# Table functions in halves between copies, loads and transposes by token pairs, doubled coefficients, a split last group: one change to a two-head kernel

## The chip, the core and the metric

The kernel runs on one core of a Trainium2 chip. The metric is the time of one execution in microseconds of the device. A run of the kernel before is the median of its executions; one of its executions was taken with the hardware profiler, and all rows below come from that one.

## The reference, cut to what matters

Two independent heads work on 2048 tokens of width 448, and their outputs are put side by side.

```python
# head A: attention of each token over 8 tokens, 2 apart, 16 heads of 28
q, k, v = (x @ wqkv).reshape(B, S, 3, H, Dh) ...
idx = pos[:, None] - off[None, :]            # off = 0, 2, ..., 14; below 0 is masked
logits = einsum("bhsd,bhswd->bhsw", q, k[idx]) * scale
a = einsum("bhsw,bhswd->bhsd", softmax(logits), v[idx]).reshape(B, S, D) @ wo
# head B: a diagonal complex state space, P = 448
Lam_bar = exp(exp(log_dt) * Lam);  B_bar = ((Lam_bar - 1) / Lam)[:, None] * Bmat
h[t] = Lam_bar * h[t-1] + B_bar @ x[t]
b = 2 * real(Cmat @ h) + x * Dskip
out = concatenate([a, b], -1)
```

## The kernel before, in words

**Head A.** Partition p holds the 16 neighbouring tokens 16p to 16p+15 (`J = 16`; "token j" below is the j-th of each partition). x is loaded into `xnA` (in the buffer u1) in four groups of four tokens, 448 KB each, by `load_x` (L104). `g_xta` (L288) transposes a group on TensorE, 16 transposes into two PSUM banks, and VectorE copies each bank to `xTA` (L296). `proj(t, j)` (L300) makes q (t = 0), k (1) or v (2) of one token: 4 matmuls (L303) and a ScalarE copy (L307). The 14 tokens before a partition's first come from the partition before by DMAs from SBUF to SBUF, `halo` (L545). `logits` (L436) works for one half of the tokens (hf = 1: tokens 8 to 15) and two of the 8 offsets at a time: a product of q and k over 7168 elements (`mul`, L445), and sums over the 28 columns (`half` L448, `quarter` L451, after every second one `rest` L454 to L457). `softmax` (L469) has a first and a second part. `pv_mul` (L503) multiplies the weights with v, four tokens and one offset at a time, into one of 7 buffers; `av` (L511) adds over offsets and transposes on TensorE, 16 matmuls with the identity (L519) into four PSUM banks, which are copied out after the eighth offset (L526, L528). `wo_j` (L531) is the output projection of one token. The four groups of tokens run from 12..15 down to 0..3; `wo_j` of a group runs between the `av` of the next.

**Head B.** The recurrence is cut into 256 chunks of 8 steps (`T = 8`), real and imaginary parts on two halves of the partitions. `params_in` and `params1` to `params3` (L218 to L266) compute powers of Lam_bar from three small loads (`prow`) and one of Dskip. `blocks` (L202) multiplies the pattern `dup` of two unit matrices with coefficients that are broadcast over the last axis: `build_R` makes one of 7 rotation matrices R (128x896), `build_G` the two that scale B, which lie in R[5] and R[6]. `tables` (L282) makes cos and sin of the chunk angle for 1792 elements: three VectorE passes in float32 scratch in u1 (L283, L196, L197), then Sin, Abs and Sin on ScalarE (L198 to L200). `b_weights` (L311), `b_x` (L320; the copies of even steps on VectorE, L327, of odd ones on ScalarE) and `c_weights` (L333) prepare operands. `ssm_in` (L353) runs the 8 steps in a chunk, for the first four of seven column groups (hf = 0) and then the last three (hf = 1). It begins with step 0, which reads the last xT copy that `b_x` makes. `scan_mul` (L372), `scan_pe` (L379), `scan_run` (L391), `scan_mul`, `scan_pe`, `scan_out` rotate into the frame of a chunk, scan over chunks and rotate back. `ssm_mix` (L403) spreads the result over the steps and `ssm_out` (L416) projects it.

**Order.** Each engine runs its instructions in the order in which the program issues them; nothing moves them afterwards. TensorE's order is the text's. Most VectorE work of head A and of the parameters goes through a list, `todo`, as pairs of a cost and a function (`add`). `pe(cost)` and `dve(cost)` keep two running sums, `load[0]` for TensorE and `load[1]` for VectorE, and `pump` takes work off the list while VectorE's sum is below TensorE's. So the costs written in the text decide in front of which b_x copies, scans and rotations a product lands. `need` takes off all that is before an item. At the start, 44 matmuls of the identity (L134) run while x is on its way. The PSUM pool has 8 banks, given out in turn. Loads, halos and stores are issued by SP in the text's order; the small parameter loads by ScalarE.

```python
def pump(lead=0.0):
    while todo and load[1] < load[0] + lead and (todo[0][2] is None or todo[0][2]()):
        pop()
```

Of the kernel before, what the change touches and what calls it, by code (L numbers as in the profile page):

```python
# [19 lines left out]
KT = 112  # L20
T = 8
# [15 lines left out]
def kernel(  # L37
# [29 lines left out]
    def bank(dt=F32):  # L67
        return psum.tile([128, 512 if dt == F32 else 1024], dt, tag="b", name="b")
# [34 lines left out]

    def load_x(jg):  # L104
        SP.dma_start(xnA[:, 4 * jg:4 * jg + 4, :], xA_r[:, 4 * jg:4 * jg + 4, :])

    def half_rows(src):
        return src.rearrange("(t i) d -> i t d", i=HS)

    load_x(3)  # L110
    load_w(1)
    load_x(2)
    load_x(1)
    load_w(0)
    load_x(0)
    prow = const.tile([3 * NT, 2, HS], BF16, tag="prow")
# [15 lines left out]
    warm = bank()  # L132
    for _ in range(44):
        PE.matmul(warm[:, 0:128], ident[:], ident[:], start=True, stop=True)  # L134
# [20 lines left out]
    todo = []  # L155
    load = [8.0, 8.0]

# [17 lines left out]
    def pe(cost):  # L175
        load[0] += cost
        pump()

    def dve(cost):
        load[1] = max(load[1], load[0]) + cost  # L180
# [5 lines left out]
    def tt(o, a_, b_, op):  # L186
        V.tensor_tensor(o, a_, b_, op)
        return o
# [6 lines left out]
    def sincos(sin_out, cos_out, y, tmp):  # L195
        V.tensor_scalar(tmp, y, 1.0, MAGIC, ALU.mult, ALU.add)  # L196
        V.scalar_tensor_tensor(tmp, tmp, -MAGIC, y, ALU.add, ALU.subtract)  # L197
        ACT.activation(sin_out, tmp, ACTF.Sin, scale=-2 * PI * SHR)  # L198
        ACT.activation(tmp, tmp, ACTF.Abs)
        ACT.activation(cos_out, tmp, ACTF.Sin, bias=hpib[:], scale=-2 * PI * SHR)  # L200

    def blocks(o, c, n):  # L202
        shp = (128, n, 2, HS)
        V.tensor_tensor(o.rearrange("p m (a b) -> p m a b", a=2), dup.unsqueeze(1).to_broadcast(shp),  # L204
                        c.unsqueeze(3).to_broadcast(shp), ALU.mult)

# [5 lines left out]
    nr, t0, den, gre, gim = [pt_(n) for n in ("nr", "t0", "den", "gre", "gim")]  # L212
    coef = const.tile([128, T - 1, NT, 2], BF16, tag="coef")
    cg = pt_("cg", (128, NT, 2))
    cgb = const.tile([128, 2, NT, 2], BF16, tag="cgb")
    kkb = kk.unsqueeze(2).to_broadcast(PW)
# [24 lines left out]

    def params2():
        tt(sn[:], sn[:], rk[:], ALU.mult)
        V.tensor_copy(coef[0:HS, :, :, 1], sn[0:HS, 0:T - 1])
        V.tensor_scalar(coef[HS:128, :, :, 0], sn[HS:128, 0:T - 1], -1.0, None, ALU.mult)
        tt(cs[:], cs[:], rk[:], ALU.mult)
        V.tensor_copy(coef[0:HS, :, :, 0], cs[0:HS, 0:T - 1])
        V.tensor_copy(coef[HS:128, :, :, 1], cs[HS:128, 0:T - 1])

    def params3():  # L250
        a1, b1 = cs[:, 0], sn[:, 0]
        V.tensor_scalar(nr[:], a1, -1.0, None, ALU.add)
        tt(gre[:], nr[:], lre, ALU.mult)
        tt(t0[:], b1, lim, ALU.mult)
        tt(gre[:], gre[:], t0[:], ALU.add)
        tt(gre[:], gre[:], den[:], ALU.mult)
        tt(gim[:], b1, lre, ALU.mult)
        tt(t0[:], nr[:], lim, ALU.mult)
        tt(gim[:], gim[:], t0[:], ALU.subtract)
        tt(gim[:], gim[:], den[:], ALU.mult)  # L260
        V.tensor_copy(cg[0:HS, :, 0], gre[0:HS])
        V.tensor_copy(cg[0:HS, :, 1], gim[0:HS])
        V.tensor_scalar(cg[HS:128, :, 0], gim[HS:128], -1.0, None, ALU.mult)
        V.tensor_copy(cg[HS:128, :, 1], gre[HS:128])
        V.tensor_copy(cgb[:, 0], cg[:])
        tt(cgb[:, 1], cg[:], cgb[:, 0], ALU.subtract)  # L266

    def build_G():
        blocks(G.rearrange("p r t n -> p (r t) n"), cgb.rearrange("p r t a -> p (r t) a"), 2 * NT)

# [6 lines left out]

    ftab = u1.bitcast(F32)
    yy = ftab[:, 0:NT * NC].rearrange("p (t c) -> p t c", t=NT)
    tm = ftab[:, NT * NC:2 * NT * NC].rearrange("p (t c) -> p t c", t=NT)  # L280

    def tables():  # L282
        V.tensor_tensor(yy, iot.unsqueeze(1).to_broadcast((128, NT, NC)),  # L283
                        fT.unsqueeze(2).to_broadcast((128, NT, NC)), ALU.mult)
        sincos(tab[:, 1], tab[:, 0], yy, tm)


    def g_xta(jg):  # L288
        for k2 in range(2):
            tp = bank(BF16)  # L290
            tpv = tp[0:KT].rearrange("p (k j n) -> p k j n", k=2, j=4)
            for kk_ in range(2):
                for jj in range(4):
                    kt = 2 * k2 + kk_
                    PE.transpose(tpv[:, kk_, jj, :], xnA[:, 4 * jg + jj, KT * kt:KT * (kt + 1)], ident[:])
            V.tensor_copy(xTA[:, 2 * k2:2 * k2 + 2, 4 * jg:4 * jg + 4, :], tpv)  # L296
            dve(0.69)
            load[0] += 0.45

    def proj(t, j):  # L300
        ps = bank()
        for kt in range(4):
            PE.matmul(ps[:, 0:D], xTA[:, kt, j, :], wts[:, t, kt, :], start=(kt == 0), stop=(kt == 3))  # L303
        src = ps[:, 0:D].rearrange("p (h d) -> p d h", h=H)
        dst = (q_s[:, :, j * H:(j + 1) * H] if t == 0 else
               k_s[:, :, HALO + j, :] if t == 1 else v_s[:, HALO + j])
        ACT.copy(dst, src)  # L307
        pe(0.76)

# [186 lines left out]
    out_a = out[0].rearrange("(p j) n -> j p n", j=J)  # L496
    steps = [(n_, jg, s) for n_, jg in enumerate((3, 2, 1, 0)) for s in range(W)]
    count = [0, 0]

    def pv_of(i):  # L500
        return late[:, 1792 * (i % NPV):1792 * (i % NPV + 1)].rearrange("p (j d h) -> p j d h", j=JG, d=DH)

    def pv_mul(i):  # L503
        _, jg, s = steps[i]
        V.tensor_tensor(pv_of(i), attn[:, s, JG * H * jg:JG * H * (jg + 1)].rearrange("p (j h) -> p j h", h=H)  # L505
                        .unsqueeze(2).to_broadcast((128, JG, DH, H)), v_s[:, 2 * s + JG * jg:2 * s + JG * jg + JG], ALU.mult)
        count[0] += 1
# [3 lines left out]
    def av(i):  # L511
        n_, jg, s = steps[i]
        if s == 0:
            accs[n_] = [bank() for _ in range(4)]
        acc = accs[n_]
        pvf = pv_of(i).rearrange("p j d h -> p j (d h)")
        for kt in range(4):
            for jj in range(JG):
                PE.matmul(acc[kt][0:KT, jj * 128:(jj + 1) * 128], pvf[:, jj, KT * kt:KT * (kt + 1)], ident[:],  # L519
                          start=(s == 0 and jj == 0), stop=(s == W - 1 and jj == JG - 1))  # L520
        count[1] += 1
        if s == W - 1:
            for kt in range(4):
                o, a_ = oTs[n_ % 3][:, kt], acc[kt][0:KT].rearrange("p (j n) -> p j n", j=JG)
                if n_ == 3 and kt % 2 == 1:
                    V.tensor_copy(o, a_)  # L526
                else:
                    ACT.copy(o, a_)  # L528
        pe(0.92)

    def wo_j(n_, jj):  # L531
        j = JG * (3 - n_) + jj
        ps = bank()
        for kt in range(4):
            PE.matmul(ps[:, 0:D], oTs[n_ % 3][:, kt, jj, :], wo_p[:, kt, :], start=(kt == 0), stop=(kt == 3))  # L535
        ya = outp.tile([128, D], BF16, tag="yo")
        if n_ == 3 and jj % 2 == 1:
            V.tensor_copy(ya[:], ps[:, 0:D])
        else:
            ACT.copy(ya[:], ps[:, 0:D])  # L540
        SP.dma_start(out_a[j, :, 0:D], ya[:])
        pe(0.76)
# [6 lines left out]

    g_xta(3)  # L550
    params_in()
    add(1.6, params1)
    add(1.2, params2)
    add(2.5, params3)
    has_G = add(2.0, build_G)
    has_R = [add(1.0, lambda: build_R(0))]
    for j in (15, 14, 13, 12):
        proj(1, j)
    g_xta(2)
    for j in (11, 10, 9):  # L560
        proj(1, j)
    g_xta(1)
    for j in (8, 7, 6):
        proj(1, j)
    g_xta(0)
    has_tab = add(6.2, tables)
    has_D = add(0.6, build_D)
    for j in range(15, 7, -1):
        proj(0, j)
# [12 lines left out]
    for k in range(1, T - 1):  # L582
        has_R.append(add(1.0, lambda k=k: build_R(k)))
    halo(lambda lo, hi, a_, b_: v_s[lo:hi, a_:b_])
# [11 lines left out]
    for j in range(T):  # L596
        if j == 1:
            need(has_R[0])
        ssm_in(0, j)
    need(has_tab)  # L600
    scan_mul(0)
    for t2 in range(4):
# [27 lines left out]
    has_wo = add(0.0, wo_load)  # L630
    for i in range(32):
        add(1.09, lambda i=i: pv_mul(i), lambda: count[0] < count[1] + NPV)

# [8 lines left out]

    for i in range(32):
        while count[0] <= i:
            pop()
        pump(7.0)
        av(i)
        n_, _, s = steps[i]
        if n_ > 0 and s % 2 == 1:
            wo_j(n_ - 1, s // 2)  # L650
    for jj in range(JG):
        wo_j(3, jj)

# [28 lines left out]
```

## Time and profile before

| what | value |
|---|---|
| median of 3 runs (lowest, highest) | 183.68 us (183.63, 184.69) |
| profiled execution: own time | 183.74 us |
| its span, first to last instruction | 182.0 us |
| mean granted TensorE clock | 0.979 |
| TensorE: projections L303, 192 matmuls | 41.5 us busy |
| TensorE: L519, 512 matmuls | 32.3 us |
| VectorE: products L445, 8 of 3.89 us | 31.1 us |
| VectorE: L505, 32 of 1.09 us | 32.2 us |
| ScalarE: L198, L199, L200 | 1.70, 1.70, 1.79 us |

The stages, by the start of what begins them: first projection at 7.88 us, tables (L283) at 22.77, first product (L445) at 35.01, first `ssm_in` matmul at 62.78, first C transpose (L340) at 79.94, last `ssm_out` matmul at 133.57, first L519 at 135.83, last L535 at 178.49, end at 182.0.

How to read the profile: a row of the waits names the engine and line that waited, the engine and line that released it, the sum in us, how often, and the longest. A row of the timeline gives start, busy time, engine, line, operation, operands and shapes, and in brackets the idle time ahead of it with its releaser. A row of stages gives for each engine the busy time and the number of instructions; then the granted TensorE clock (1.00 is full rate), the busy share of the DMA engines and GB/s.

### The profile page before, as it was taken

How to read it: one execution, taken by the hardware profiler on the slowest of the kernel's cores; microseconds unless marked ns; L12 is line 12 of the kernel's file. 1: busy time of each engine (PE TensorE's matmuls, PEld its weight loads, DVE VectorE, ACT ScalarE, POOL GpSimd, SP SyncE). 2: the span in 40 equal slices, each digit the busy share in tenths (PEclk: the TensorE clock that was granted, in tenths of full speed). 3: DMA queues.
4: the chain of work that ended last, by engine and by line, in shares of the span. 5: the costliest groups of instructions: out<-in, count | busy, mean ns of one | idle time of the engine just before them, and what ended most of it. 6: DMA issues, size and time to landing. Idle time of an engine off the chain costs nothing.

```text
span 182.0 us, 3801 instructions
## 1 busy us (share of the span) xinstructions
PE 167.4 (92%) x1596; PEld 123.2 (68%) x1596; DVE 150.3 (83%) x172; ACT 95.8 (53%) x180; POOL 2.8 (2%) x22
## 2 busy tenths in 40 slices
PE   6968996599999899999999899999959999999992
PEld 7745652256667688887886565656539988888860
DVE  1358992399997899999999999999999999996031
ACT  2093538977787544443468955447720224426151
POOL 3000000000000000000000010000000000000000
PEclk9999999789999999999999999999996999999999
DMA  5999940059469100000000002111222001011113
GB/s 169 314 261 262 338 86 0 0 116 171 73 132 199 26 4 0 0 4 0 0 4 0 0 25 72 58 50 50 79 78 86 4 25 58 32 48 52 54 50 101
DMA packets 13135, 14.01 MB, mean 77 GB/s; under 512 B 4527, under 2 KB 12223, under 8 KB 12991
## 3 DMA queue, kind: packets, MB, share of 16 engines
q1 hardware_dynamic: 13047, 13.77, 29.6%
q8 instruction: 12, 0.20, 0.4%
q14 instruction: 5, 0.04, 0.1%
q10 hardware_dynamic: 71, 0.01, 0.0%
HBM read 6.89 MB, written 3.67 MB: 58 GB/s over the span
## 4 chain that ended last, share of the span: by engine, by line
DVE 41%; PE 39%; DMA 10%; ACT 4%; issue 3%; SPq 1%; ACTq 0%; DVEq 0%
PE b L519 17%; PE b L303 12%; DVE u L445 11%; DMA u<-in_B_x_dram 7%; PE b L535 7%; DVE u L448 4%; DVE R L204 4%; DVE l L451 3%; DMA prow<-in_B_log_dt_dram 3%; DVE u L394 2%; PE b L325 2%; PE b L315 2%; DVE l L454 2%; DVE wbuf L375 1%; DVE wbuf L376 1%
## 5 line engine op out<-in xcount | busy, mean ns | idle before, releaser
L303 PE MATMUL b<-wbuf,u 112*128 112x448 bf16 x192 | 41.5, 363 | 5.9 <-ACT q_s L307 3.7
L445 DVE TENSOR_TENSOR u<-q_s,k_s 128x7168 bf16<-128x7168 bf16 x8 | 31.1, 3888 | 6.7 <-ACT q_s L307 6.5
L519 PEld LDWEIGHTS <-k_s 128*112 128x112 bf16 x512 | 32.0, 135 | 4.1 <-DVE k_s L505 2.4
L519 PE MATMUL b<-ident,k_s 128*112 128x128 bf16 x512 | 32.3, 225 | 2.3 <-DVE k_s L505 2.3
L303 PEld LDWEIGHTS <-u 112*128 112x128 bf16 x192 | 18.1, 100 | 22.4 <-issue 5.9
L505 DVE TENSOR_TENSOR k_s<-u,v_s 128x1792 bf16<-128x1792 bf16 x32 | 32.2, 1089 | 0.4 <-PE b L519 0.4
L360 PE MATMUL b<-xT,BT 112*128 112x256 bf16 x224 | 26.9, 272 | 0.8 <-DVE xT L327 0.8
L367 ACT CAST u<-b 128x512 bf16<-128x512 f32 (+1 forms) x32 | 15.6, 535 | 18.4 <-PE b L366 14.8
L360 PEld LDWEIGHTS <-BT 112*128 112x128 bf16 x224 | 21.7, 98 | 4.0 <-DVE xT L327 0.9
L420 PE MATMUL b<-Cw,u 128*128 128x448 bf16 x112 | 23.8, 352 | 0.0
L540 ACT CAST ya<-b 128x448 bf16<-128x448 f32 x14 | 7.5, 538 | 18.0 <-PE b L535 13.3
L448 DVE TENSOR_TENSOR u<-u 128x3584 bf16<-128x3584 bf16 x8 | 16.2, 2023 | 0.2
L420 PEld LDWEIGHTS <-u 128*128 128x128 bf16 x112 | 10.5, 98 | 7.5
L424 ACT CAST yo<-b 128x448 bf16<-128x448 f32 x16 | 8.6, 537 | 11.5 <-PE b L422 8.7
L535 PE MATMUL b<-u,q_s 112*128 112x448 bf16 x64 | 14.1, 352 | 0.0
L528 ACT CAST q_s<-b 112x512 bf16<-112x512 f32 x14 | 7.2, 596 | 11.7 <-PE b L519 11.7
L411 ACT CAST u<-b 128x512 bf16<-128x512 f32 (+1 forms) x28 | 13.1, 558 | 0.2 <-PE b L410 0.2
L307 ACT CAST v_s<-b 128x448 bf16<-128x448 f32 x16 | 8.5, 532 | 3.3 <-PE b L303 3.3
L307 ACT CAST k_s<-b 128x448 bf16<-128x448 f32 x16 | 7.9, 552 | 4.4 <-PE b L303 4.4
L410 PE MATMUL b<-u,R 128*128 128x255 bf16 x49 | 9.5, 272 | 0.7 <-ACT u L401 0.7
L307 ACT CAST q_s<-b 128x448 bf16<-128x448 f32 x16 | 8.2, 535 | 3.5 <-PE b L303 3.5
L408 PE MATMUL b<-u,ident 128*128 128x512 bf16 (+1 forms) x28 | 9.9, 353 | 0.0
(119 smaller groups left out, 184.1 us busy)
## 6 DMA issues: line engine op xcount, KB each, us to landing
u<-in_A_x_dram SPq DMA_DIRECT2D x4, 448.0 KB, 6.3
u<-in_B_x_dram SPq DMA_DIRECT2D x2, 896.0 KB, 16.9
out_dram<-yo SPq DMA_DIRECT2D x16, 112.0 KB, 1.7
out_dram<-ya SPq DMA_DIRECT2D x16, 112.0 KB, 1.7
wbuf<-in_A_wqkv_dram SPq DMA_DIRECT2D x3, 392.0 KB
k_s<-k_s SPq DMA_DIRECT2D x1, 784.0 KB
v_s<-v_s SPq DMA_DIRECT2D x1, 784.0 KB
k_s<-k_s SPq DMA_DIRECT2D x1, 588.0 KB
```

Of the source, the lines that this page charges most:

```text
L303: PE.matmul(ps[:, 0:D], xTA[:, kt, j, :], wts[:, t, kt, :], start=(kt == 0), stop=(kt == 3))
L307: ACT.copy(dst, src)
L360: PE.matmul(ps[:, i * NC:(i + 1) * NC], BT[:, kt, t, :], xT[:, kt, j, :], start=(kt == 0 and i == 0), stop=(kt == 3 and j == 0 and i == le ...
L367: ACT.copy(Z[:, pr_[0]:pr_[0] + n, j, :], ps[:, 0:n * NC].rearrange("p (t c) -> p t c", t=n))
L408: PE.matmul(ps[:, 0:n * NC], ident[:], Z[:, sl, j, :], start=True, stop=False)
L411: ACT.copy(Z[:, sl, j, :], ps[:, 0:n * NC].rearrange("p (t c) -> p t c", t=n))
L420: PE.matmul(ps[:, 0:D], Z[:, t, j, cols], Cw[:, t, :], start=(t == 0), stop=False)
L445: V.tensor_tensor(pr[:], qv, kv, ALU.mult)
L448: V.tensor_tensor(pr[:, :, 0:14, :], pr[:, :, 0:14, :], pr[:, :, 14:28, :], ALU.add)
L505: V.tensor_tensor(pv_of(i), attn[:, s, JG * H * jg:JG * H * (jg + 1)].rearrange("p (j h) -> p j h", h=H) .unsqueeze(2).to_broadcast((128, ...
L519: PE.matmul(acc[kt][0:KT, jj * 128:(jj + 1) * 128], pvf[:, jj, KT * kt:KT * (kt + 1)], ident[:], start=(s == 0 and jj == 0), stop=(s == W ...
L535: PE.matmul(ps[:, 0:D], oTs[n_ % 3][:, kt, jj, :], wo_p[:, kt, :], start=(kt == 0), stop=(kt == 3))
```

## The change

- **Loads.** `load_x(lo, hi)` takes any range of tokens. Tokens 14, 15 come first, then the k weights, 12, 13, then 8 to 11 and 4 to 7, the q weights, and 0 to 3: five loads instead of four.
- **Transposes by pairs.** `g_xta(jp)` does two tokens: 8 transposes in one bank and one copy. Eight calls stand between the projections. The warming matmuls go from 44 to 34.
- **Tables.** The scratch moves from u1 into the table itself and R[1..4]. The VectorE passes stay whole. The three functions are cut into a part of 1024 and one of 768 elements, and the six go into a list, `acts`, from which `proj` takes one after every second copy.
- **Doubled coefficients.** `coef` and `cgb` hold each coefficient twice, side by side, and `blocks` reads them, `dup` and the output with a last axis of two. R[0] is now built ahead of G.
- **Last group.** The last four tokens become two groups of two. `pv_mul` of these works on 896 elements, `av` makes 8 matmuls into two banks, and `wo_j` of the group before is spread accordingly.
- **Costs.** The starting sums of `load` go from 8 to 6, `build_R` from 1.0 to 0.5 and 0.6, `build_G` from 2.0 to 1.0, `pv_mul` to 0.15+0.235 per token.

On VectorE the order changes at two places behind this. Before, the last xT copy (step 0) comes ahead of the product of the first offsets for hf = 0; now it comes after it. Before, `scan_run` of hf = 1 comes after a `quarter`; now after a product.

```diff
-    load_x(3)
+    load_x(14, 16)
     load_w(1)
-    load_x(2)
-    load_x(1)
+    load_x(12, 14)
+    load_x(8, 12)
+    load_x(4, 8)
     load_w(0)
-    load_x(0)
+    load_x(0, 4)
...
-    for _ in range(44):
+    for _ in range(34):
...
-    load = [8.0, 8.0]
+    load = [6.0, 6.0]
...
     def blocks(o, c, n):
-        shp = (128, n, 2, HS)
-        V.tensor_tensor(o.rearrange("p m (a b) -> p m a b", a=2), dup.unsqueeze(1).to_broadcast(shp),
-                        c.unsqueeze(3).to_broadcast(shp), ALU.mult)
+        shp = (128, n * 2, HS // 2, 2)
+        V.tensor_tensor(o.rearrange("p m (a b e) -> p m a b e", a=2, e=2),
+                        dup.rearrange("p a (b e) -> p a b e", e=2).unsqueeze(1).to_broadcast((128, n, 2, HS // 2, 2)),
+                        c.unsqueeze(3).to_broadcast((128, n, 2, HS // 2, 2)), ALU.mult)
...
-    coef = const.tile([128, T - 1, NT, 2], BF16, tag="coef")
+    coef = const.tile([128, T - 1, NT, 2, 2], BF16, tag="coef")
...
-    ftab = u1.bitcast(F32)
-    yy = ftab[:, 0:NT * NC].rearrange("p (t c) -> p t c", t=NT)
-    tm = ftab[:, NT * NC:2 * NT * NC].rearrange("p (t c) -> p t c", t=NT)
+    yy = tab.rearrange("p a t c -> p (a t c)").bitcast(F32).rearrange("p (t c) -> p t c", t=NT)
+    tm = R[:, 1:5].rearrange("p k t n -> p (k t n)").bitcast(F32).rearrange("p (t c) -> p t c", t=NT)
...
-        sincos(tab[:, 1], tab[:, 0], yy, tm)
+        V.tensor_scalar(tm, yy, 1.0, MAGIC, ALU.mult, ALU.add)
+        V.scalar_tensor_tensor(tm, tm, -MAGIC, yy, ALU.add, ALU.subtract)
+        for t in (slice(0, 4), slice(4, NT)):
+            acts.append(lambda t=t: ACT.activation(tab[:, 1, t], tm[:, t], ACTF.Sin, scale=-2 * PI * SHR))
+            acts.append(lambda t=t: ACT.activation(tm[:, t], tm[:, t], ACTF.Abs))
+            acts.append(lambda t=t: ACT.activation(tab[:, 0, t], tm[:, t], ACTF.Sin, bias=hpib[:], scale=-2 * PI * SHR))
...
+    def g_xta(jp):
+        tp = bank(BF16)
+        tpv = tp[0:KT].rearrange("p (k j n) -> p k j n", k=4, j=2)
+        for kt in range(4):
+            for jj in range(2):
+                PE.transpose(tpv[:, kt, jj, :], xnA[:, 2 * jp + jj, KT * kt:KT * (kt + 1)], ident[:])
+        V.tensor_copy(xTA[:, :, 2 * jp:2 * jp + 2, :], tpv)
+        dve(0.69)
+        load[0] += 0.45
...
         ACT.copy(dst, src)
+        count[2] += 1
+        if acts and count[2] % 2 == 0:
+            acts.pop(0)()
         pe(0.76)
...
-    steps = [(n_, jg, s) for n_, jg in enumerate((3, 2, 1, 0)) for s in range(W)]
-    count = [0, 0]
+    groups = ((12, 4), (8, 4), (4, 4), (2, 2), (0, 2))
+    steps = [(n_, s) for n_ in range(len(groups)) for s in range(W)]
...
-    g_xta(3)
+    g_xta(7)
     params_in()
...
-    has_G = add(2.0, build_G)
-    has_R = [add(1.0, lambda: build_R(0))]
-    for j in (15, 14, 13, 12):
-        proj(1, j)
+    has_R = [add(0.5, lambda: build_R(0))]
+    has_G = add(1.0, build_G)
+    for jp in (6, 5, 4, 3):
+        proj(1, 2 * jp + 3)
+        proj(1, 2 * jp + 2)
+        g_xta(jp)
+    proj(1, 7)
     g_xta(2)
-    for j in (11, 10, 9):
-        proj(1, j)
-    g_xta(1)
-    for j in (8, 7, 6):
-        proj(1, j)
-    g_xta(0)
+    proj(1, 6)
     has_tab = add(6.2, tables)
     has_D = add(0.6, build_D)
-    for j in range(15, 7, -1):
+    proj(0, 15)
+    g_xta(1)
+    proj(0, 14)
+    g_xta(0)
+    for j in range(13, 7, -1):
         proj(0, j)
...
-        has_R.append(add(1.0, lambda k=k: build_R(k)))
+        has_R.append(add(0.6, lambda k=k: build_R(k)))
...
-    for i in range(32):
-        add(1.09, lambda i=i: pv_mul(i), lambda: count[0] < count[1] + NPV)
+    for i in range(len(steps)):
+        add(0.15 + 0.235 * groups[steps[i][0]][1], lambda i=i: pv_mul(i), lambda: count[0] < count[1] + NPV)
```

## The prediction, made before the changed kernel ran

> **What bounds the kernel now.** I read the busy times, then the slices, the waits, the chain, and last the stages around each wait.
>
> ```profile
> PE 167.4 (92%) x1596; PEld 123.2 (68%) x1596; DVE 150.3 (83%) x172; ACT 95.8 (53%) x180; POOL 2.8 (2%) x22
> ...
> PEclk9999999789999999999999999999996999999999
> ```
>
> TensorE is busy in 92% of the span. Two slices have a low clock. The waits say what stands before both:
>
> ```profile
> DVE u L445 <- ACT q_s L307: 6.5, 1, 6.5
> PE b L303 <- ACT q_s L307: 3.7, 1, 3.7
> PE b L519 <- DVE k_s L505: 2.3, 1, 2.3
> PE b L360 <- DVE xT L327: 0.8, 1, 0.8
> ```
>
> The 6.5 and 3.7 us are one event. ScalarE works on the table functions and copies nothing:
>
> ```profile
> 24.82 1.09 DVE L196 TENSOR_SCALAR u<-u 128x1792 f32<-128x1792 f32 x1
> 28.01 1.70 ACT L198 ACTIVATE tab<-u 128x1792 bf16<-128x1792 f32 x1 [3.44 <-DVE u L197]
> 33.16 1.81 ACT L307 CAST q_s<-b 128x448 bf16<-128x448 f32 x4
> 35.01 3.89 DVE L445 TENSOR_TENSOR u<-q_s,k_s 128x7168 bf16<-128x7168 bf16 x1 [6.50 <-ACT q_s L307]
> ```
>
> From 62.78 to 133.57 TensorE runs almost without a gap, and VectorE beside it; from 135.83 on the chain is TensorE. In stages of one microsecond a gap in TensorE's work shows its second price:
>
> ```profile
> 35.00:36.00 1.00, 1.00 (x4) 0.37 (x3) 0.99 (x1) 1.00 (x3) 0.00 (x0) 0.50 0.00 0
> ...
> 137.00:138.00 1.00, 1.00 (x11) 1.00 (x11) 1.00 (x2) 0.00 (x0) 0.00 (x0) 0.50 0.31 76
> ```
>
> The column before the last two is the granted clock. Summed over its slices, each of the two stretches loses 1.70 us (0.29+0.50+0.50+0.41; 0.09+3x0.50+0.11). They follow idle times of 3.7 and 2.26 us; idle times of 2.06 us (from 12.2) and 0.8 us (62.0) are followed by none.
>
> Two places will decide. The first is the start of the state-space stage; the second is its second half:
>
> ```profile
> 62.03 0.69 DVE L327 COPY xT<-b 112x1024 bf16<-112x1024 bf16 x1 [0.60 <-PE b L325]
> 62.64 3.88 DVE L445 TENSOR_TENSOR u<-q_s,k_s 128x7168 bf16<-128x7168 bf16 x1
> 62.78 3.67 PE L360 MATMUL b<-xT,BT 112*128 112x256 bf16 x32 [0.79 <-DVE xT L327]
> ...
> 98.40 0.55 DVE L376 TENSOR_TENSOR wbuf<-u,tab 128x768 bf16<-128x768 bf16 x1
> 98.86 1.08 DVE L451 TENSOR_TENSOR l<-u 128x1792 bf16<-128x1792 bf16 x1
> 99.87 1.84 DVE L394 TENSOR_TENSOR_SCAN u<-rk,b 128x256 bf16<-128x256 f32 x3
> 102.21 0.55 DVE L376 TENSOR_TENSOR wbuf<-u,tab 128x768 bf16<-128x768 bf16 x1
> 102.95 0.38 PE L385 MATMUL b<-wbuf,ident 128*128 128x512 bf16 x1
> ```
>
> TensorE waits for the last xT copy, and later L385 starts 0.2 us after VectorE's rotated product is ready. Both times a short VectorE job stands ahead: there is no slack.
>
> **The change part by part.** I walk the changed instruction order with these rows' durations and compare five stages.
>
> *1, start to tables (22.77 now).* Ten warming matmuls fewer (0.105 us each) free TensorE at 4.9 instead of 6.0. The first load is half as large. A first projection needs the small parameter rows, which stand ahead of it on TensorE; they land about 6.3 to 7.5, so it starts near 6.85 instead of 7.88. But now each pair of projections waits for its own transposes: 8 transposes (0.45), 0.2 until VectorE starts, its 0.69 copy, 0.05. That idles TensorE 0.94 us, four times, and VectorE's small parameter work fills these gaps. A pair takes 1.51+1.39 = 2.9. The second pair starts at 9.85, since VectorE's chain of 1.8 us from the parameters (8.78 to 10.60 now, 1.5 earlier) stands ahead of its copy; the next at 12.75, 15.7 and 18.6. Then come the transposes of tokens 4 and 5, q15 and the next transposes, whose copy ends at 22.7: the tables start. So the half-size transposes eat the earlier start. G with 1.09 instead of 2.01 is in this chain and counted; if it stayed 2.01, add 0.75.
>
> The other bound: the warming matmuls run at 105 ns, the same 128 columns later at 56 (1.79 us for 32). The first projections ran at 190 ns each, so the rate rose at about 7.5. With 34 and then a gap it may rise only after the first pair, and two projections and eight transposes take 1.9 us more: 24.6. Nothing tells which; I take 23.6, +0.85.
>
> *2, tables to state space (40.0 now: 22.77 to 62.78).* VectorE needs 5.2 as before. ScalarE's three functions become six. The 1024-wide Exp took 1.07, the 1792-wide Sin 1.70, so a 768 costs 0.86: 5.97 in all against 5.19. Two copies of 0.455 stand between. VectorE's three passes (5.25), Sin and two copies, Abs and two copies come before the first product: 5.25+1.07+0.91+1.07+0.91 = 9.25 after the tables' start instead of 12.24: 3 us gained on VectorE. TensorE loses its 3.7 us wait and the first slow clock. But ScalarE finishes the k copies 10.5 after it began, 38.5 instead of 37.6, and TensorE, eight banks ahead, waits for banks until v token 10: 39.05, against about 41.3. The 11.05 us of v projections and B weights follow, ending at 50.1 against 52.34: 2.25 ahead.
>
> That lead is then lost. In the new order VectorE has xT6, half, xT4, quarter, xT2, **product**, xT0; before, the product came after xT0. xT2 comes 7.45 after 50.1; then 0.6+3.92+0.7 pass before L360: 62.85. TensorE has finished its transposes at 59.75 (8 pairs of 1.21) and idles 3.1 us. In tables' terms 40.15: +0.15.
>
> *3, state space, first half (17.2).* TensorE's own time, plus the clock. An idle 3.1 lies between the 2.06 that cost nothing and the 3.7 that cost 1.70. Bounds 0 and 1.70; I take 1.70, since the 2.26 cost it already. The row is what I go by. The Trainium skill, TensorE: Matmul & The Clock Gate, section Why this matters for your kernels, allows idle gaps of up to about 3 us between bursts; the trace disagrees, for 2.26 us was followed by a slow stretch. By that rule this gap is on the edge and the one in stage 4 free, and the sum would lie between +0.15 and +1.85; by the trace's 2.26 it is +1.85 at least. The same section asks for at least 4 us of unbroken work before full rate, which speaks against cutting the warming.
>
> The doubled coefficients belong here. The R build reads a coefficient broadcast over the last axis: 896 elements in 1084 ns, while L505 does 1792 in 1089 with a last axis of 16 in order. With pairs I take half the rate term: 0.62 (nearest: L275, 448 slow elements, 617 ns); the upper bound is 1.08. Six builds save 2.8 or nothing. VectorE is ahead there anyway: 62.85+15.2 = 78, and must wait for ScalarE's copy at T+1.0, that is 81.0 or later (T is TensorE's first C transpose, now 79.94). The saving is worth nothing on the path; were they slow, VectorE would come at 80.9, still on time. This cover holds.
>
> *4, T to the attention matmuls (55.9 now).* VectorE from T+1.0: rotation 1.2, C weights 2.14, quarter 1.1, four scans 2.34, rotation 1.3, product 3.92, half 2.04, quarter 1.12, rest 2.4: T+18.6. Rotation until 19.6; then a **product** of 3.85 ahead of the scans (now a quarter of 1.1), 23.45; scans 1.76; rotation, 25.8 and 26.3. TensorE reaches L385 at T+23.5 and waits 2.3 there, and about 0.6 before. It leaves at 26.8 instead of 23.66: +3.1. Its end of stage is 53.63+3.1 = T+56.75. VectorE has softmax done at about T+53, so the 2.26 us wait is gone: +0.85. Bounds of the added clock price: 0 and 1.70; two thirds of such a gap must fall as it did at 133.57, so I leave it out.
>
> *5, attention to the end (46.17 now).* 160 matmuls in 10.85 become 8.95 at 0.0559: no slow stretch, and VectorE has products in hand. TensorE's count is the same, so the smaller last group gains only the acc copies: two instead of four, but one output matmul group less covers them: +0.2. VectorE pays 16x0.62-8x1.09 = +1.2, beside TensorE, which it leads by over 3 us; without that lead, 1.2. Sum -1.7.
>
> SP: one load more, 0.33 to 0.49 of issue; later loads have over 10 us to spare. The k halo is issued with k2's copy, about 11 after the functions' start, as before near 36.7, and its traffic lasts 11.5; the third product comes 1.3 after it, hidden.
>
> Sum: +0.85+0.15+1.70+0.85-1.70 = +1.85. The profiled execution took 183.74 (span 182.0), the median is 183.68: 185.6.
>
> **Rivals.**
>
> *VectorE's saving arrives.* VectorE is 100% busy from 35 to 131, which speaks for it. If the products in front of xT0 and the scans held up nobody, state space would start at 60.6 (-2.2), the 2.26 us wait would go (-2.27), and the clock (-1.7): 177.6. It decides if the xT0 copy starts by 60. The order speaks against.
>
> *A near tie:* no slow stretch and an early full clock at the start: 183.74+0-0.86+0.15 = 183.0, 182.4 if the parameter rows land at 6.3. For it: gaps of 2.06 us cost nothing.
>
> *Both gaps slow TensorE and the start is slow:* 185.6+1.7+1.0 = 188.3. For it: a 2.26 us gap did.
>
> *The pairs bring no rate:* only G counts, +0.75, inside the range.
>
> **How the numbers follow.** Saving arrives 0.08; near tie 0.32; forecast 0.40 (184.7 with an early clock to 186.6); both gaps 0.20. Within 1%, what a measurement here can tell from none, is 181.8 to 185.5: the near tie and a quarter of the forecast, 0.43. Faster 0.10, with 0.02 for what I miss; slower 0.47, the rest. Range 182.4 to 188.3: it leaves out the first rival.
>
> **What would show it.** Tables at 22.7 to 24.6. First product 9.3 after. xT0 copied after a 3.9 us product, TensorE idle some 3 us, then a half clock. R builds at 0.62. L385's wait of 2 us near T+23.5. No wait before the attention matmuls. I am wrong if xT0 comes before the product, if TensorE passes L385 without waiting, or if the half-size transposes do not idle TensorE.

## The result, and the profile after

| | before | after |
|---|---|---|
| median us (lowest, highest), 20 runs each on one chip | 183.54 (182.62, 185.92) | 184.38 (183.32, 186.35) |
| ratio after to before, 95% interval | | 1.0053 (1.0030 to 1.0075) |
| profiled execution: own time, span | 183.74, 182.0 | 184.28, 182.5 |
| mean granted clock | 0.979 | 0.972 |

The change makes the kernel 0.84 us slower, where 1.92 was forecast (185.6 against 183.68). Several kernels below have single executions about 2 us above their others, which the ratios leave out; the profiled ones of the first kernel of experiment 3 and of "pairs alone" are such.

The five stages of the prediction, each from the start of what begins it (us):

| stage | before | predicted | after | after less before |
|---|---|---|---|---|
| start to tables | 22.77 | 23.6 | 22.14 | -0.63 |
| tables to state space | 40.0 | 40.15 | 38.76 | -1.25 |
| state space, first half | 17.16 | 18.86 | 19.92 | +2.76 |
| T to attention | 55.9 | 56.75 | 57.38 | +1.48 |
| attention to end | 46.17 | 44.47 | 44.3 | -1.87 |

The sum is +0.5, as the spans have it. The page of the kernel after, busy times and granted clock:

```profile
PE 167.1 (92%) x1584; PEld 121.9 (67%) x1586; DVE 146.9 (80%) x179; ACT 95.2 (52%) x184; POOL 2.8 (2%) x22
...
PEclk9999999999999579999999978999999999999999
```

VectorE has 3.4 us less work than before and is busy in 80% of a longer span, not 83%: the saving became idle time. Both stretches of low clock that the kernel before had are gone; two others have come. The waits of the kernel after say what stands ahead of them:

```profile
PE b L372 <- DVE xT L339: 3.8, 1, 3.8
PE b L397 <- DVE wbuf L387: 2.3, 2, 2.1
PE b L312 <- ACT v_s L316: 0.3, 1, 0.3
```

And those of VectorE:

```profile
DVE wbuf L387 <- ACT u L379: 6.4, 1, 6.4
DVE u L457 <- ACT q_s L316: 2.7, 1, 2.7
```

The wait of 3.7 us for ScalarE's q copies is gone (0.3 us for a v copy is left of TensorE's waits for ScalarE there), and VectorE's 6.5 has shrunk to 2.7. VectorE's longest wait is now 6.4 us, for ScalarE ahead of the first rotation. TensorE now waits 3.8 us for the last xT copy and 2.1 us for the rotated product instead. The timeline of the kernel after at the first place:

```profile
55.76 0.68 DVE L339 COPY xT<-b 112x1024 bf16<-112x1024 bf16 x1
...
56.37 3.88 DVE L457 TENSOR_TENSOR u<-q_s,k_s 128x7168 bf16<-128x7168 bf16 x1
...
60.16 0.68 DVE L339 COPY xT<-b 112x1024 bf16<-112x1024 bf16 x1
...
60.90 1.46 PE L372 MATMUL b<-xT,BT 112*128 112x256 bf16 x6 [3.76 <-DVE xT L339]
```

VectorE starts a product of 3.88 us at 56.37 and copies xT[0] only after it; TensorE has nothing else to do from 57.14 to 60.90. This product is the fourth of the profile, so it is the last one of tokens 8 to 15 (`logits(1, 3, 0)`), and not one of hf = 0 as the section on the change has it. The stages around it, with the granted clock third from the end:

```profile
59.00:60.00 1.00, 0.00 (x0) 0.00 (x0) 1.00 (x1) 0.00 (x0) 0.00 (x0) 0.88 0.00 0
60.00:61.00 1.00, 0.10 (x1) 0.10 (x2) 1.00 (x3) 0.00 (x0) 0.00 (x0) 0.50 0.00 0
62.00:63.00 1.00, 1.00 (x6) 0.70 (x5) 0.97 (x2) 0.17 (x1) 0.00 (x0) 0.50 0.00 0
...
66.00:67.00 1.00, 1.00 (x8) 0.80 (x7) 1.00 (x3) 0.00 (x0) 0.32 (x3) 0.71 0.00 0
67.00:68.00 1.00, 1.00 (x12) 0.89 (x10) 1.00 (x3) 0.42 (x1) 0.00 (x0) 1.00 0.00 0
```

The clock is halved during the wait already, and for 6.8 us in all: a row at 0.88 has been at half clock for 0.24 us of its one, then come six whole rows, and the row at 0.71 adds 0.58. At half clock a row holds 6 to 8 matmuls, at 67.00 it holds 12. The second place, on VectorE and on TensorE:

```profile
100.18 3.88 DVE L457 TENSOR_TENSOR u<-q_s,k_s 128x7168 bf16<-128x7168 bf16 x1
103.98 1.83 DVE L406 TENSOR_TENSOR_SCAN u<-rk,b 128x256 bf16<-128x256 f32 x3
105.85 0.56 DVE L387 TENSOR_TENSOR wbuf<-u,tab 128x768 bf16<-128x768 bf16 x1
...
106.47 0.39 PE L397 MATMUL b<-wbuf,ident 128*128 128x512 bf16 x1 [2.08 <-DVE wbuf L387]
```

Another product stands ahead of the scans, TensorE waits 2.08 us, and the clock is halved from 107.5 to 111.0.

### The profile page after: what moved, and what is told of

It reads as the page before. It is cut to its first block, busy times and chain, and to the rows that moved or that the text cites. A ratio compares the mean times of both kernels' runs of the same rounds, so it can differ in the third digit from the quotient of the medians.

```text
span 182.5 us, 3794 instructions
## 1 busy us (share of the span) xinstructions
PE 167.1 (92%) x1584; PEld 121.9 (67%) x1586; DVE 146.9 (80%) x179; ACT 95.2 (52%) x184; POOL 2.8 (2%) x22
## 3 DMA queue, kind: packets, MB, share of 16 engines
HBM read 6.89 MB, written 3.67 MB: 58 GB/s over the span
## 4 chain that ended last, share of the span: by engine, by line
PE 58%; DVE 32%; ACT 7%; issue 1%; POOL 0%; DVEq 0%; POOLq 0%; ACTq 0%
PE b L537 16%; PE b L432 12%; DVE u L457 11%; PE b L372 9%; PE b L554 7%; PE b L312 4%; DVE u L460 3%; DVE l L463 2%; DVE u L406 2%; DVE u L305 2%; PE b L135 2%; PE b L434 2%; PE b L378 2%; PE b L304 2%; PE b L422 2%
## 5 line engine op out<-in xcount | busy, mean ns | idle before, releaser
L312 PE MATMUL b<-wbuf,u 112*128 112x448 bf16 x192 | 40.0, 353 | 4.1 <-DVE u L305 3.8
L520 DVE TENSOR_TENSOR k_s<-u,v_s 128x1792 bf16<-128x1792 bf16 (+1 forms) x40 | 33.6, 897 | 4.8 <-PE b L537 4.8
L372 PE MATMUL b<-xT,BT 112*128 112x256 bf16 x224 | 29.7, 290 | 3.9 <-DVE xT L339 3.8
L537 PEld LDWEIGHTS <-k_s 128*112 128x112 bf16 x512 | 30.6, 130 | 2.0
L537 PE MATMUL b<-ident,k_s 128*112 128x128 bf16 x512 | 30.9, 219 | 0.0
L312 PEld LDWEIGHTS <-u 112*128 112x128 bf16 x192 | 17.6, 97 | 18.4 <-DVE u L305 4.4
L372 PEld LDWEIGHTS <-BT 112*128 112x128 bf16 x224 | 23.1, 104 | 8.3 <-DVE xT L339 3.9
L432 PE MATMUL b<-Cw,u 128*128 128x448 bf16 x112 | 24.9, 364 | 0.0
L559 ACT CAST ya<-b 128x448 bf16<-128x448 f32 x15 | 8.1, 537 | 16.8 <-PE b L554 13.4
L305 DVE COPY u<-b 112x1024 bf16<-112x1024 bf16 x8 | 5.5, 690 | 6.6 <-PE b L304 6.6
```

The source lines that it names most:

```text
L372: PE.matmul(ps[:, i * NC:(i + 1) * NC], BT[:, kt, t, :], xT[:, kt, j, :], start=(kt == 0 and i == 0), stop=(kt == 3 and j == 0 and i == le ...
L432: PE.matmul(ps[:, 0:D], Z[:, t, j, cols], Cw[:, t, :], start=(t == 0), stop=False)
L520: V.tensor_tensor(pv_of(i), attn[:, s, H * j0:H * (j0 + nj)].rearrange("p (j h) -> p j h", h=H) .unsqueeze(2).to_broadcast((128, nj, DH, H ...
L537: PE.matmul(acc[kt // kb][0:KT, o:o + 128], pvf[:, jj, KT * kt:KT * (kt + 1)], ident[:], start=(s == 0 and o == 0), stop=(s == W - 1 and o ...
```

## The experiments

The theory: the new operations save time; the order that the planner makes from the new cost numbers puts two products where TensorE waits for what stands behind them, and this takes back more than was saved. The rival: the new operations save nothing on TensorE's path, whatever the order. Before was measured again with each group of kernels (183.72, 183.56, 183.50).

### 1. xT[0] ahead of the product

```diff
-        add(3.9, mul)
+        add(3.9, mul, None if after is None else (lambda: after in free))
...
-    logits(1, 3, 0)
+    logits(1, 3, 0, "xT")
...
         proj(0, j)
         b_x(j)
+    free.add("xT")
+    pop()
+    load[1] += -1.29
```

The product waits in the list until its name is in `free`. `pop()` then takes it off at once, and `load[1]` is corrected so that the order behind it stays that of the kernel after.

> The changed kernel with one product moved behind the last xT copy; all else, the scans behind a product too, in the changed kernel's order. Theory (two products hold TensorE up): the state space starts at about 57.9 instead of 60.90 (-3.0) and the half clock behind that gap goes (-2.76), so -5.8: about 178.6 us against 184.4 for the changed kernel; L397's wait of 2 us before the second rotation stays. Rival (VectorE is the bound and TensorE's wait at xT0 is slack): the 5.8 come back as a wait before the attention matmuls, and the time stays within 1 us of 184.4.

Measured: 177.87 us, ratio 0.9682 (0.9622 to 0.9742). The timeline:

```profile
56.91 0.69 DVE L339 COPY xT<-b 112x1024 bf16<-112x1024 bf16 x1 [0.73 <-PE b L337]
57.52 3.88 DVE L459 TENSOR_TENSOR u<-q_s,k_s 128x7168 bf16<-128x7168 bf16 x1
...
57.66 3.67 PE L372 MATMUL b<-xT,BT 112*128 112x256 bf16 x32 [0.78 <-DVE xT L339]
```

The same two jobs of VectorE in the other order: the first 32 step matmuls take 3.67 us, not 6.42, and start 3.24 earlier. The medians differ by 6.5 us (184.38 less 177.87). In the profiled executions it is 7.2 us, and 5.7 of them stand at this place, as expected: tables to state space takes 35.78 us (38.76), the first half 17.16 (19.92). Another 1.2 lie at the second place: its wait of 2.09 us is still there, but in this execution no half clock follows it (T to attention 56.18, not 57.38). Two of the four executions do have a half clock somewhere (0.989 on average, the others 1.000), and they take 1.4 us more.

### 2. The second half's scans ahead of the product

```diff
-        logits(0, n_, g)
+        logits(0, n_, g, "scan" if n_ == 2 else None)
...
     scan_run(banks)
     scan_mul(1)
+    free.add("scan")
```

> The changed kernel with only the other product moved, behind the scans and the second rotation of the last three column groups. Theory: L397's wait of 2.1 us goes and the half clock behind it (0.9 net): -3.0, about 181.4 us, with the 3.8 us wait at xT0 and its half clock untouched; TensorE then reaches the attention matmuls with VectorE's softmax only just done. Rival (softmax is the bound): less than 1 us comes off, and a wait stands before the attention matmuls.

Measured: 180.74 us, ratio 0.9835 (0.9763 to 0.9906). The wait for wbuf is 0.2 us, and T to attention takes 53.86 us, not 57.38: the second place is worth 3.5 us by the stage and 3.6 by the medians (184.38 less 180.74). TensorE's 3.76 us wait at the steps is the same, but was followed by a half clock of only 3.4 us.

### 3. Both

Both products are held as in experiments 1 and 2.

```diff
+    free.add("xT")
...
+    free.add("scan")
```

> Both products moved. Theory: the two add up, -8.8, about 175.6 us, no TensorE wait over 1 us behind the first projections and no half clock after the start. Rival (VectorE the bound): no better than the better of the two alone.

Measured: 178.27 us, ratio 0.970 (0.9644 to 0.9755): a miss by 2.7 us, and no better than the first alone. Here `pop()` and the correction of `load[1]` were missing, so the order behind moved by one place: a `half` of 2.02 us, and not a `quarter` of 1.08, came ahead of the first half's scans. A wait was back, now ahead of the second half's first rotation:

```profile
PE b L397 <- DVE wbuf L387: 2.3, 1, 2.3
```

With the order behind kept exactly (both edits above as they stand):

> The kernel after with two products held: the one ahead of xT[0] until xT[0] is copied, and the one ahead of the second half's scans until its second rotation; the rest of VectorE's order as in the kernel after. Theory (both waits cost by themselves, each with a half clock of its own): 177.9 less 2.8 is about 175.1, no half clock, no wait of over 1 us at the step products or the scans' transposes. Rival (VectorE is the bound behind the first wait, the second is made good ahead of the attention products): 177.3 to 178.3, with a wait before the attention products in place of the one at the scans.

Measured: 176.30 us, ratio 0.9622 (0.9550 to 0.9694). Of the 2.8 us, 1.6 are left. TensorE has no wait of over 0.8 us from the tables to the end, and there is no half clock before the end of its work. Its profiled execution took 178.04 us, with the late start that experiment 8 shows. The expected rival, a wait ahead of the attention matmuls, did not show.

### 4. The gap filled

```diff
+    fill = bank()
+    for _ in range(60):
+        PE.matmul(fill[:, 0:128], ident[:], ident[:], start=True, stop=True)
+
     for j in range(T):
         if j == 1:
```

Sixty matmuls of the identity, read by nobody, lie ahead of step 0 of the first half. The product stays ahead of xT[0].

> The changed kernel with 60 matmuls of the identity (3.4 us at 56 ns) in TensorE's gap before the state space; they compute nothing that is used. Order on VectorE untouched, so the state space still starts near 61. Theory: only the clock's part of the price goes, -2.8, about 181.6 us. Rival (the gap costs its idle time alone and the half clock is hidden by other waits): no change from 184.4.

Measured: 181.89 us, ratio 0.9907 (0.9867 to 0.9947). The steps start no earlier, but run at full clock:

```profile
61.25 3.67 PE L372 MATMUL b<-xT,BT 112*128 112x256 bf16 x32 [0.41 <-DVE xT L339]
```

So of the 5.7 us of experiment 1's first place, 2.5 (medians) to 2.8 (first half, 19.92 less 17.16) are the clock, and the rest is the wait.

### 5. The old cost numbers, all new operations kept

```diff
-    load = [6.0, 6.0]
+    load = [8.0, 8.0]
...
-    has_R = [add(0.5, lambda: build_R(0))]
-    has_G = add(1.0, build_G)
+    has_R = [add(1.0, lambda: build_R(0))]
+    has_G = add(2.0, build_G)
...
-        has_R.append(add(0.6, lambda k=k: build_R(k)))
+        has_R.append(add(1.0, lambda k=k: build_R(k)))
```

VectorE's products, xT copies and scans are then in the order of the kernel before.

> The kernel after with the planner's four numbers set back (load 8.0, 8.0; a build of R 1.0; of G 2.0). All changed operations stay; the order of VectorE's products, xT copies, scans and rotations is then that of the kernel before. Theory (the order that the new numbers give, and not the new operations, costs the time: the product ahead of xT[0] 6.5 us and the product ahead of the scans 3 us, partly one in the place of the other; the operations gain 6.3 us by the tables and 1.4 us by the coefficients, and lose about 2 us by the pairs at the start): 176.5 to 178.5, no wait of 3.8 us at the step products and none of 2.1 us at the scans' transposes. Rival (the operations themselves leave the state space no earlier than in the kernel after): 182 to 184.

Measured: 177.40 us, ratio 0.9649 (0.9585 to 0.9714). Its page and waits:

```profile
PEclk9999999999999999999999999999999999999999
```

```profile
PE b L537 <- DVE k_s L520: 1.9, 1, 1.9
PE b L372 <- DVE xT L339: 0.8, 1, 0.8
```

No operation differs from the kernel after, only five numbers of the planner do, and 7.0 us are gone (184.38 to 177.40). The rival (182 to 184) is out.

### 6. Doubled coefficients alone, on the kernel before

VectorE's order is that of before.

```diff
-    coef = const.tile([128, T - 1, NT, 2], BF16, tag="coef")
+    coef = const.tile([128, T - 1, NT, 2, 2], BF16, tag="coef")
...
-    cgb = const.tile([128, 2, NT, 2], BF16, tag="cgb")
+    cgb = const.tile([128, 2, NT, 2, 2], BF16, tag="cgb")
```

with `blocks` and what fills both as in the change.

> The kernel before with one part of the change alone: the coefficients stored doubled, so the rotation builds G (1) and R (7) run over (NT, 32, 2) in pairs. VectorE's order of work is that of the kernel before. In the kernel after, a build of 896 elements took 0.62 us where it took 1.08. Theory (the VectorE time saved is worth something only where TensorE waits for VectorE: the G build of about 0.9 us lies before the product that delays the state space, and the builds of R ahead of the scans shorten a wait for wbuf of 2.3 us): 1 to 2.5 us faster, about 182.0. Rival (VectorE waits for the step products anyway, so nothing on the path): 183.4 to 183.9.

Measured: 182.12 us, ratio 0.9889 (0.9816 to 0.9962), -1.44. The tables start 0.86 us earlier (21.91), mostly by the saving on G; some of it can be the spread of the start, for in experiment 7, with the old G, they start 0.25 earlier. Six rotation builds save 2.8 us. VectorE spends 1.8 of them waiting for ScalarE ahead of the rotation, and 0.4 reaches TensorE (its wait ahead of attention is 1.85, not 2.26).

### 7. Tables in halves alone, on the kernel before

```diff
-    ftab = u1.bitcast(F32)
+    yy = tab.rearrange("p a t c -> p (a t c)").bitcast(F32).rearrange("p (t c) -> p t c", t=NT)
+    tm = R[:, 1:5].rearrange("p k t n -> p (k t n)").bitcast(F32).rearrange("p (t c) -> p t c", t=NT)
...
         ACT.copy(dst, src)
+        copies[0] += 1
+        if acts and copies[0] % 2 == 0:
+            acts.pop(0)()
```

> The kernel before with one part alone: the table functions in a scratch buffer of their own, in halves between ScalarE's projection copies. VectorE's order is that of the kernel before. Theory: the first product starts some 3 us earlier because u is free of the tables and its q copies no longer stand behind four whole table functions, the state space starts at about 60.5 us of the span as in the kernel after, but with xT[0] copied before the next product there is no 3.8 us wait and no half clock there: 2 to 4 us faster, about 180.5. Rival (the earlier product alone makes the state space wait, whatever the order of VectorE): 183 to 185, with a wait of over 2 us ahead of the step products.

Measured: 177.25 us, ratio 0.9649 (0.9576 to 0.9723). The timeline at the same places:

```profile
29.70 3.89 DVE L454 TENSOR_TENSOR u<-q_s,k_s 128x7168 bf16<-128x7168 bf16 x1 [1.44 <-ACT q_s L313]
...
56.26 0.69 DVE L336 COPY xT<-b 112x1024 bf16<-112x1024 bf16 x1 [0.60 <-PE b L334]
56.87 3.88 DVE L454 TENSOR_TENSOR u<-q_s,k_s 128x7168 bf16<-128x7168 bf16 x1
57.01 3.67 PE L369 MATMUL b<-xT,BT 112*128 112x256 bf16 x32 [0.79 <-DVE xT L336]
```

The state space starts 5.77 us earlier than before, and that is the 3.67 us wait for ScalarE, the 1.70 that the half clock behind it lost, and 0.4, of which 0.25 is the earlier start of the tables. Another 0.8 us comes at the end: the wait ahead of the attention matmuls is still 2.26 us, but no half clock follows it (45.39 us from there, not 46.17). This part alone brings 6.3 us in the medians: most of it is the stall before the first product. I had expected 2 to 4.

### 8. Loads and transposes by pairs alone, and 44 warming matmuls in the kernel after

On the kernel before, with `g_xta` as in the change and its calls between the projections:

```diff
-    load_x(3)
+    load_x(14, 16)
...
-    for _ in range(44):
+    for _ in range(34):
...
-    g_xta(3)
+    g_xta(7)
```

> The kernel before with one part alone: x loaded and transposed by token pairs, 34 warming matmuls instead of 44. Theory: the gain of the start seen in the kernel after (the tables start at 22.1 us of the span instead of 22.8) is all that this part does: 0.4 to 0.9 us faster, about 183.1. Rival (the pairs move VectorE's transposes so that something later waits, as their count and durations enter the planned order): 0.5 us or more slower, with a new wait of TensorE between the transposes of the middle groups.

Measured: 185.90 us, ratio 1.0120 (1.0092 to 1.0148): slower, as the rival said. TensorE does wait between the transposes, 0.79 us four times, where the kernel before waits 2.06 once; the kernel after has the same four waits. The larger part is another. TensorE's first rows, in the profiled execution of 187.60 us:

```profile
4.97 1.06 PE L294 MATMUL b<-ident,u 128*112 128x128 bf16 x8
...
6.81 3.17 PE L302 MATMUL b<-wbuf,u 112*128 112x448 bf16 x8 [0.58 <-DVE u L295]
9.77 1.06 PE L294 MATMUL b<-ident,u 128*112 128x128 bf16 x8
11.62 0.55 PE L302 MATMUL b<-wbuf,u 112*128 112x448 bf16 x2 [0.79 <-DVE u L295]
```

and in that of the kernel after:

```profile
4.97 0.70 PE L304 MATMUL b<-ident,u 128*112 128x128 bf16 x8
...
6.46 1.69 PE L312 MATMUL b<-wbuf,u 112*128 112x448 bf16 x8 [0.63 <-DVE u L305]
7.98 0.61 PE L304 MATMUL b<-ident,u 128*112 128x128 bf16 x8
9.38 1.69 PE L312 MATMUL b<-wbuf,u 112*128 112x448 bf16 x8 [0.79 <-DVE u L305]
```

The same instructions after the same warming: in one execution the rate rises at 5 us, in the other only after 10, and the second pair of tokens comes 2.24 us later (11.62 less 9.38). Of eight profiled kernels with 34 warming matmuls three show the late rise. With that taken off, the tables of this kernel would start at 24.3 (26.57 less 2.24), still 1.6 after the kernel before and 2.2 after the kernel after (22.14). These 2.2 are VectorE's order: the seventh copy of the transposes stands at 23.76, or 21.5 without the late rise, as in the kernel after (21.53); but here the eighth copy (24.97) and the old R build of 1.1 us (25.58) come ahead of the tables, and there neither does. The wait of 5.03 us for q, with 6.8 us of half clock, adds little: tables to state space is 40.23 us, 0.2 more than before. So in this execution 3.8 of 3.9 us are lost ahead of the tables. How the 2.3 us of the median divide between late rise and order is not settled, as no row tells when the rate rose in the other nine.

The kernel after with 44 again:

```diff
-    for _ in range(34):
+    for _ in range(44):
```

> The kernel after with 44 warming matmuls in place of 34. Theory (the rise of TensorE's rate comes at a time of its own: in some executions with 34 at the first transposes, near 5 us, in others only near 10 us, which makes the first tables 2.2 us later; with 44 it comes ahead of the projections in all of them, and the start pays 1.06 us for ten more): 184.0 to 185.2, with the slowest executions closer to the fastest, and the tables at 23.0 to 23.4 us of the span. Rival (the rise comes early with 34 as well, ten more only cost): 185.4, with the same spread.

Measured: 184.79 us (183.35 to 185.93), ratio 1.0070 (1.0029 to 1.0111). The tables start at 23.36 us, as expected, but the median is within 0.4 us of the kernel after, and the spread is 2.6 us in 10 executions where that has 3.0 in 20: inconclusive.

### 9. The split last group alone, and the two parts that pay

The split group on the kernel before:

```diff
-    steps = [(n_, jg, s) for n_, jg in enumerate((3, 2, 1, 0)) for s in range(W)]
+    groups = ((12, 4), (8, 4), (4, 4), (2, 2), (0, 2))
+    steps = [(n_, s) for n_ in range(len(groups)) for s in range(W)]
```

with `pv_mul`, its costs, `av` and `wo_j` as in the change.

> The kernel before with one part alone: the last token group in two parts of two tokens each. Theory: no gain that can be seen, as the work after the last attention product is the same in sum: 183.4 to 184.0. Rival A (the shorter last piece brings the end of ScalarE's and VectorE's tail forward): 0.5 to 1.0 us faster, and the last 8 us of the span show a shorter tail behind TensorE. Rival B (more, smaller steps): 0.5 us slower.

Measured: 183.46 us, ratio 0.9963 (0.9926 to 1.0000): no gain that can be told from none.

Tables in halves and doubled coefficients, the diffs of experiments 6 and 7 together, on the kernel before, with its loads, transposes, groups and order:

> The kernel before with two parts of the change: table functions in halves in a scratch buffer, and doubled coefficients; loads, transposes, last group and VectorE's order as before. Theory (the tables' 6.3 us stay; of the coefficients' 1.4 us the part ahead of the first product stays, and with TensorE at full rate the saving on the rotations shortens the wait ahead of the attention products, 2.26 us with the tables alone): 175.0 to 176.5, the fastest of all. Rival (the coefficients' gain was of the same wait that the tables remove): 177.0 to 177.6.

Measured: 176.52 us, ratio 0.9622 (0.9559 to 0.9685). With the order held exactly (experiment 3, second kernel) it is the fastest; the two cannot be told apart.

The parts alone measure -6.3, -1.4, +2.3 and -0.1, in sum -5.5 us. All together in the old order measure -6.1 (experiment 5). So the operations add up within 0.6 us, though the +2.3 holds late rises and an order of its own, and the +7.0 from experiment 5 to the kernel after is the order's.

## Why the prediction was right and where it failed

The mechanism stands: the product ahead of xT[0], the product ahead of the scans, a half clock behind a wait, the wait ahead of attention gone, and VectorE's saving on R worth next to nothing on the path (0.4 us reach TensorE in experiment 6). The sum was too high by 1.3 us. Two steps failed it: the terms of stages 1 and 2 were together 2.9 us too high. That it came out as near as it did is luck, for stages 3 and 4 were 1.7 too low.

- **Stage 1, "I take 23.6, +0.85": measured -0.63.** The step that failed is the time of the rate's rise. I took a value between both bounds; in this execution the rise came at 5.15 us. TensorE also reached the parameter rows at 5.61, not 6.3, so the projections began at 6.46, not 6.85. The four stalls came as worked out: 1.40 us from the start of the transposes to the next projection, where the sum had 0.45 and 0.94. Kernels with 34 warming matmuls have both starts, as experiment 8 shows (with the late one the tables stand at 24.24 and 24.38 in the two kernels of experiment 3), so 24.6 was a real bound.
- **Stage 2, "TensorE, eight banks ahead, waits for banks until v token 10: 39.05": measured a wait of 0.29 us, ending at 37.51.** The step that failed is the time of ScalarE's k copies, "10.5 after it began": it measured 8.8 (27.38 to 36.21), since the sixth function runs behind them and the recorded times of neighbouring ScalarE jobs overlap by 0.1 us. So the banks came free early, the v stage ended at 48.25, not 50.1, and stage 2 became 1.25 us shorter where I had +0.15. The rest held: product at xT2, xT[0] behind it, a wait of 3.76 where I had 3.1.
- **Stage 3, "Bounds 0 and 1.70; I take 1.70": measured 2.76.** The upper bound was wrong. The half clock lasted 6.8 us, two pieces of 3.4, and began 1.1 us before the steps. The rows of before, with one piece behind 3.67 us, told of no second piece; the last section shows where it comes from.
- **Stage 4, "I leave it out": measured a half clock of 3.4 us behind the 2.08 us wait.** The stage was 0.63 longer than forecast. The waits were right (2.08 and 0.20 for 2.3 and 0.6), and experiment 1 shows the stage without the half clock: 56.18. Leaving the term out rested on "two thirds of such a gap must fall as it did at 133.57", for which no row was given. Over all runs, waits of 1.85 to 2.26 us were free of a half clock in 8 of 17.
- **Stage 5, -1.7: measured -1.87.** Right: 160 matmuls in 9.10, as TensorE had no wait ahead of them.

The first rival, "VectorE's saving arrives", had 177.6 as its time and "if the xT0 copy starts by 60" as its condition, with "the order speaks against". Where the order was set right, the condition and the time both came: xT[0] at 56.91 and 177.87 us in experiment 1, 177.40 in experiment 5. That the time fits is in part luck: in experiment 1 the state space starts 5.1 us earlier than before, where the rival had 2.2, and T to attention is 0.3 longer, where it had 2.27 less. Its "100% busy" VectorE was busy for 92.66 of the 96 us from 35 to 131. The rivals "near tie" (183.0) and "both gaps slow TensorE and the start is slow" (188.3) each had one right part: the early start of the near tie, and the slow second gap of the other.

The Trainium skill, TensorE: Matmul & The Clock Gate, section Why this matters for your kernels, allows idle gaps of up to about 3 us. The runs differ: 9 of 17 waits of 1.85 to 2.26 us were followed by half clock. The seven longer ones (3.20 to 5.03) all were, as that page has it, and waits of 0.8 never.

## What to carry to other kernels

When a change makes operations cheaper and a planner orders work by their costs, look at what the new order puts directly ahead of the short jobs that another engine waits for: here a 0.7 us copy behind a 3.9 us product cost some 6 us, about all that the operations saved in the old order (6.1). Measure the new operations in the old order first, one part at a time; four parts of this change measured -6.3, -1.4, +2.3 and -0.1 us. Price a wait of TensorE as the wait and the clock behind it, each as a range: for a wait near 2 us the second was nothing or one piece of half clock, for one near 4 us one piece or two.

## What the runs showed of the hardware

- The half clock came in pieces of 3.4 us (1.70 us of TensorE's work lost where it was busy throughout). Seven waits of 3.20 us or more were all followed by it: three by two pieces (3.76, 3.76 and 5.03 us), four by one (3.20, 3.67, 3.67 and 3.76).
- What decides is where a wait lies. The trace records the granted clock as stretches, and in each of the 14 traces all of them begin on a grid of 3.413 us: in the kernel after at 59.76 and 107.55, 14 steps apart; in the split group alone at 14.66, 35.14 and 137.54, 6 and 30 steps apart. With each execution divided into slices along its grid, TensorE's idle time (us) in the slices of a wait is:

| wait | idle time per slice | half clock after |
|---|---|---|
| 2.26 us, kernel before | 2.26 | one piece |
| 2.26 us, experiment 7 | 1.50, then 0.76 | none |
| 3.76 us, kernel after | 2.62, then 1.14 | two pieces |
| 3.76 us, experiment 2 | 0.49, then 3.28 | one piece |

Of 686 slices at full clock, all 28 with 1.85 us of idle time or more were followed by half clock (12 of them at the end of TensorE's work), and none with 1.80 or less. Of 19 slices at half clock, the three with 0.97 or more were followed by another, the 16 with 0.29 or less by full clock. The grid lies differently in each execution (its first border at 0.2 to 3.4 us), so the same wait can cost nothing in one execution and a piece in the next. These limits are read from the traces; no kernel was built to test them.

- The rise of the rate at the start lies on the same grid. The record of the clock begins at the rise; in the rows of stages the time before it shows as 1.00, so there only the durations tell: eight projection matmuls take 3.17 us before it and 1.69 after it. With 34 warming matmuls the rise came at 4.6 to 6.8 us in five executions and at 10.4 to 10.7 in three, with 44 at 4.4 to 7.1 in all six. In each execution it is the end of the first slice with 0.53 us of idle time or less; in the three late ones the slice before that had 0.58.
- A VectorE build of 896 elements whose coefficient was broadcast over the last axis took 1.08 us; with each coefficient stored twice and a last axis of two, 0.62, and 1792 elements 1.08 where they took 2.01.
